# Attention by pairs of heads in halves of the matrix array, with the row maximum subtracted inside the second score product

## The chip, the cores and the metric

The kernel runs on one core of one Trainium2 chip. The metric is device time in microseconds; the kernel before takes 984.76 us (median of 3 runs, 983.75 to 986.17).

## The reference, cut to what matters

All tensors are float32. Two batches of 8 heads, 1152 keys, head dimension 64; q is pooled by pairs of rows to 576 queries per head. The weights arrive as float64.

```python
def _attn_ref(q, k, v):                       # q, k, v: (2, 8, 1152, 64)
    q_pool = q.reshape(B, H, S // 2, 2, D).mean(axis=3)
    scores = (1.0 / np.sqrt(D)) * np.matmul(q_pool, k.transpose(0, 1, 3, 2))
    scores = scores - np.max(scores, axis=-1, keepdims=True)
    attn = np.exp(scores)
    attn = attn / (np.sum(attn, axis=-1, keepdims=True) + 1e-09)
    return np.matmul(attn, v)

x = attention, heads side by side             # (1152, 512)
x = np.maximum(x @ w_in, 0) ** 2 @ w_out      # 2048 hidden units
out = ((x @ w_a) * (x @ w_b)) @ w_out2        # 1536 hidden units
```

## The kernel before

One program in two stages on one core: the attention (`attention`, L199 to L476), then the two feed-forward blocks (`mlp1`, `mlp2`), which the change leaves alone. Products are made in float32r (one pass of the matrix array per column) from operands split exactly into hi + lo, or in plain float32.

The attention works in 32 units; a unit is one head and half of its queries (CQ = 288 columns), over KT = 9 key tiles of 128. For a head, k and the pooled q are split into hi and lo side by side (`k_hi`, `k_lo`, `q_sum`, `q_hi`, `q_lo`, L254 to L274: ScalarE copies, GpSimd subtractions and additions), transposed by TensorE (`trans`, L276) into `kT`, `qB`, and `qC`, which is `qB` with its halves swapped by two GpSimd DMAs (L304, L305). So a full 128-row product of `kT` with `qB` and one with `qC` hold all the hi and lo terms of a score.

A unit's steps are: `scores` (L312), two float32r products per key tile into PSUM and a ScalarE copy of two key tiles to `s` in SBUF; `colmax` (L325), a VectorE reduction of all nine key tiles to `mx`, and a GpSimd all-reduce over the partitions to `gm`; `sub` (L340), three VectorE subtractions of `gm`; `expo` (L344), three ScalarE exponentials; `values` (L348), nine plain float32 products with 128 columns of weights, 64 of v and 64 ones, so that the denominators come out beside the values; `denom`, `recip`, `scale`, `x_hi`, `x_lo` (L359 to L392), the division and the hi/lo split of the result, once per two units.

The order is written out by hand: the table START (L23) for the beginning, then a loop over slots (L427) that issues, per slot s, the maximum of unit s + 2, the subtraction of s + 1, scores of s + 4, values of s. Each engine runs its instructions in this order, so an instruction that waits holds all behind it on its engine. `mx` has one buffer and `gm` two. SyncE issues the loads of k, q, v and of the raw weights in its own order.

`w_step` (L174) does one stage of the conversion of one weight piece, float64 words to hi and lo, on ScalarE, VectorE and, for the first pieces, GpSimd. In the attention, two pieces are begun early and the first NE = 4 are finished at the end. `early_mm` and `early_post` (L527, L533) make the first feed-forward products for half of the tokens inside the last slots of the attention; the stage after it begins with the tile `h` (L547).

Of the kernel before, what the change touches and what calls it, by code (L numbers as in the profile page):

```python
# [9 lines left out]
F32 = mybir.dt.float32  # L10
# [12 lines left out]
START = """  # L23
k_hi 0 1 A; q_sum 0 0 V; k_hi 0 0 V; k_hi 0 2 V; k_lo 0 0 P; q_hi 0 0 A; q_lo 0 0 V; q_sum 0 1 V; q_hi 0 1 A
k_lo 0 1 V; k_lo 0 2 P; trans 0 3 o AAA; q_lo 0 1 P; k_hi 1 * V; trans 0 0 t V; trans 0 1 o A
trans 0 4 o VAV; q_sum 1 * V; q_hi 1 * V; scores 0 0 A; load_q 2; k_lo 1 * P; scores 0 1 A; trans 1 2 o A
load_k 3; trans 0 2 o V; scores 0 2 A; load_k 2; load_v 2; scores 2 0 A; trans 1 1 t A; colmax 0 0
q_lo 1 * P; scores 0 3 A; scores 0 4 A; trans 1 0 t A; load_q 3; q_sum 2 * P; colmax 0 1; trans 1 3 o AVV
q_sum 3 * P; q_hi 2 * V; scores 2 1 A; scores 2 2 A; load_v 3; k_hi 3 * A; scores 2 3 A; k_lo 3 * P
k_hi 2 * V; q_lo 2 * V; load_q 4; trans 1 4 o AAV; k_lo 2 * P; scores 1 0 A; scores 2 4 A; trans 2 4 o AAA  # L30
sub 0 0; scores 1 1 A; scores 3 0 A; load_v 0; colmax 2; trans 2 3 o AAV; w_load 3; load_k 4; scores 1 2 A
trans 3 0 o A; q_hi 3 * V; scores 1 3 A; load_k 5; trans 3 2 o A; q_lo 3 * P; trans 2 2 t A; scores 3 1 A
sub 0 1; q_sum 4 * P; trans 2 0 o V; scores 1 4 A; expo 0 0; scores 3 2 A; sub 0 2; load_q 5; scores 4 0 A
trans 3 1 t A; expo 0 1; values 0 0; colmax 1; sub 2 0; scores 3 3 A; scores 3 4 A; trans 2 1 t A; expo 0 2
trans 3 3 o VVV; values 0 1; trans 3 4 o AAV; w_step 2; scores 4 1 A; values 0 2; k_hi 4 * A; sub 2 1
scores 4 2 A; values 0 3; k_lo 4 * P; expo 2 0; load_v 1; q_hi 4 * A; load_k 6; sub 2 2; values 0 4
q_lo 4 * P; colmax 3; sub 1 0; scores 5 0 A; sub 1 1; q_sum 5 * P; scores 4 3 A; expo 2 1; values 2 0
scores 5 1 A; expo 2 2; load_q 6; scores 5 2 A; values 2 1; scores 4 4 A; values 2 2; denom 0; scores 5 3 A
expo 1 0; scores 5 4 A; k_hi 5 * A; sub 1 2; values 2 3; values 2 4; w_step 2
"""  # L40
START_SLOT = 2


@with_exitstack
def kernel(
# [27 lines left out]
    TC = CQ // QP  # L73
# [9 lines left out]
    NU = NH * 2  # L83
# [7 lines left out]
    NE = 4  # L91
# [82 lines left out]
    def w_step(limit, hi=True):  # L174
        """One stage of one of the pieces before `limit`, not the one just worked on if there is another;
        one piece more may start."""
        limit = min(limit, len(order))
        if hi:
            w_hi()
        can = [i for i in sorted(work) if i < limit]  # L180
        if at["next"] < min(limit + 1, len(order)) and len(work) < 2:
            can.append(at["next"])
        if not can:
            return
        i = next((i for i in can if i != at["last"]), can[0])
        if i == at["next"]:
            at["next"] += 1
        w_stage(i)
# [10 lines left out]
    def attention(gs):  # L199
        with ExitStack() as es:  # L200
            qk_stack = ExitStack()
            qk = qk_stack.enter_context(tc.tile_pool(name="qk", bufs=1, side="right"))
            ap = es.enter_context(tc.tile_pool(name="ap", bufs=1))
            ps_s = es.enter_context(tc.tile_pool(name="ps_s", bufs=2, space=PSUM))
            ps_o = es.enter_context(tc.tile_pool(name="ps_o", bufs=3, space=PSUM))
            ps_t = es.enter_context(tc.tile_pool(name="ps_t", bufs=1, space=PSUM))

            idf = ap.tile([P, CQ], F32, tag="sg", bufs=2, name="idf")[:, :P]
            make_identity(nc, idf)
            idr = const.tile([P, P], F32R, name="idr")  # L210
            nc.vector.tensor_copy(idr, idf)
            eps = const.tile([P, 1], F32, name="eps")
            nc.vector.memset(eps, 1e-9)
            NV = 4
            vt = [ap.tile([P, 2 * KT + 1, D], F32, name=f"v{i}") for i in range(NV)]
            for i in range(NV):
                nc.gpsimd.memset(vt[i][:, 0::2, :], 1.0)

            kin, qin, khl, qhl, kT, qB, qC = {}, {}, {}, {}, {}, {}, {}
            st, om, sg, mx_t, xf, rs = {}, {}, {}, {}, {}, {}  # L220

            def k_tile(h):
                kin[h] = qk.tile([P, KT, D], F32, tag="kin", bufs=2, name=f"kin{h}")
                return kin[h], k[h // H, h % H].rearrange("(p t) d -> p t d", t=KT)

            def q_tile(h):
# [465 lines left out]
```

## Time and profile before

| | before |
|---|---|
| median of 3 runs | 984.76 us (983.75 to 986.17) |
| profiled execution, span | 983.4 us |
| busy: TensorE (PE) / VectorE (DVE) / ScalarE (ACT) / GpSimd (POOL) | 729.4 / 557.4 / 419.5 / 151.7 us |
| first product of the feed-forward stage proper (tile `h`) | 566.0 us |

The span runs from the first to the last instruction of one profiled execution. PE records of matmuls overlap, since products are pipelined: the duration of a record is a latency, and what a product costs in a dense stream is the distance from one start to the next. PEclk is the granted clock of TensorE, where 1.0 is 2.4 GHz and 0.5 is 1.2 GHz. A line of the profile names the source line, the engine, the operation, the tile written and the tiles read, the shape, the count, the busy time and the mean; in brackets or after the bar stands the idle time ahead of it with the work that ended it.

### The profile page before, as it was taken

How to read it: one execution, taken by the hardware profiler on the slowest of the kernel's cores; microseconds unless marked ns; L12 is line 12 of the kernel's file. 1: busy time of each engine (PE TensorE's matmuls, PEld its weight loads, DVE VectorE, ACT ScalarE, POOL GpSimd, SP SyncE). 2: the span in 40 equal slices, each digit the busy share in tenths (PEclk: the TensorE clock that was granted, in tenths of full speed). 3: DMA queues.
4: the chain of work that ended last, by engine and by line, in shares of the span. 5: the costliest groups of instructions: out<-in, count | busy, mean ns of one | idle time of the engine just before them, and what ended most of it. 6: DMA issues, size and time to landing. Idle time of an engine off the chain costs nothing. (4 is left out here: it accounts for less than half of the span.)

```text
span 983.4 us, 10073 instructions
## 1 busy us (share of the span) xinstructions
PE 729.4 (74%) x3830; PEld 659.7 (67%) x3830; DVE 557.4 (57%) x657; ACT 419.5 (43%) x769; POOL 151.7 (15%) x151
## 2 busy tenths in 40 slices
PE   6372757446366366357446899999999999999998
PEld 5362545335345255246335799999999999899987
DVE  7546474544635445455556789349756677127721
ACT  6353535345345344345332656237523454225510
POOL 3211322123123122123111222000000000000000
PEclk9696777867767767778677899999999999999999
DMA  5210502102003003001000122223213333103212
GB/s 151 83 48 1 115 24 49 24 25 58 14 24 73 0 25 72 1 12 37 0 1 0 43 86 87 87 84 108 68 62 105 110 128 117 57 22 116 77 33 65
DMA packets 57905, 56.36 MB, mean 57 GB/s; under 512 B 21024, under 2 KB 50400, under 8 KB 57856
## 3 DMA queue, kind: packets, MB, share of 16 engines
q1 hardware_dynamic: 55712, 51.88, 18.5%
q0 software_dynamic: 1920, 3.54, 1.7%
q8 instruction: 30, 0.49, 0.2%
q10 hardware_dynamic: 224, 0.30, 0.1%
q14 instruction: 19, 0.16, 0.0%
HBM read 49.81 MB, written 2.36 MB: 53 GB/s over the span
## 5 line engine op out<-in xcount | busy, mean ns | idle before, releaser
L333 DVE TENSOR_REDUCE mx<-s 128x288 f32<-128x2592 f32 (+1 forms) x32 | 146.8, 4587 | 235.0 <-POOL gm L338 234.7
L355 PE MATMUL o<-s,v 128*128 128x288 f32 x576 | 192.1, 463 | 8.2 <-ACT s L346 7.6
L321 PE MATMUL ps<-qB,kT 128*128 128x288 f32 x288 | 117.6, 419 | 100.9 <-ACT s L247 100.7
L321 PEld LDWEIGHTS ps<-qB,kT 128*128 128x128 f32 x288 | 63.9, 222 | 112.6 <-ACT s L247 107.6
L355 PEld LDWEIGHTS o<-s,v 128*128 128x128 f32 x576 | 118.2, 222 | 30.4 <-ACT s L346 8.3
L293 PE MATMUL pt<-idr,qhl 96*128 96x96 f32 x96 | 21.4, 348 | 105.6 <-POOL qhl L274 105.0
L346 ACT ACTIVATE s<-s 128x864 f32<-128x864 f32 x96 | 88.5, 924 | 25.1 <-DVE s L342 24.9
L342 DVE TENSOR_TENSOR s<-s,gm 128x864 f32<-128x864 f32 x96 | 96.3, 1057 | 2.6 <-POOL gm L338 2.6
L247 ACT COPY s<-ps 128x576 f32<-128x576 f32 (+1 forms) x160 | 91.6, 585 | 10.5 <-PE ps L322 8.1
L322 PE MATMUL ps<-qC,kT 128*128 128x288 f32 x288 | 92.5, 332 | 1.6 <-DVE qC L249 1.6
L293 PEld LDWEIGHTS pt<-idr,qhl 96*128 96x128 f32 x96 | 14.8, 182 | 116.1 <-POOL qhl L274 110.6
L168 DVE TENSOR_TENSOR wlo<-wx,whi 128x512 fp32r<-128x512 f32 x60 | 41.8, 696 | 54.6 <-ACT whi L134 54.5
L322 PEld LDWEIGHTS ps<-qC,kT 128*128 128x128 f32 x288 | 65.2, 226 | 6.1 <-DVE qC L249 1.8
L338 POOL PARTITION_ALL_REDUCE gm<-mx x32 | 38.5, 1202 | 191.9 <-issue 164.6
L134 ACT CAST whi<-wx 128x512 fp32r<-128x512 f32 x68 | 42.1, 620 | 55.9 <-DVE wx L153 55.8
L489 PE MATMUL y<-gl,whi 128*128 128x384 f32 x192 | 64.6, 337 | 1.2 <-DVE gl L479 1.2
L488 PE MATMUL y<-gh,whi 128*128 128x384 f32 x192 | 64.6, 336 | 0.0
L490 PE MATMUL y<-gh,wlo 128*128 128x384 f32 x192 | 64.6, 336 | 0.0
L247 ACT CAST qB<-pt 128x288 fp32r<-128x288 f32 x30 | 12.0, 401 | 117.2 <-PE pt L293 117.1
L490 PE MATMUL h<-xh,wlo 128*128 128x384 f32 (+1 forms) x176 | 57.6, 327 | 0.0
L488 PE MATMUL h<-xh,whi 128*128 128x384 f32 (+1 forms) x176 | 57.5, 327 | 0.0
L489 PE MATMUL h<-xl,whi 128*128 128x384 f32 (+1 forms) x176 | 57.5, 327 | 0.0
(92 smaller groups left out, 1590.2 us busy)
## 6 DMA issues: line engine op xcount, KB each, us to landing
raw<-in_moe_w_out_dram SPq DMA_DIRECT2D x28, 512.0 KB, 3.3
raw<-in_moe_w_in_dram SPq DMA_DIRECT2D x16, 512.0 KB, 3.8
raw<-in_moe_w_a_dram SPq DMA_DIRECT2D x12, 512.0 KB, 3.5
raw<-in_moe_w_b_dram SPq DMA_DIRECT2D x12, 512.0 KB, 3.5
v<-in_v_dram SPq DMA_DIRECT2D x16, 288.0 KB, 4.2
kin<-in_k_dram SPq DMA_DIRECT2D x15, 288.0 KB, 2.9
qin<-in_q_dram SPq DMA_DIRECT2D x15, 288.0 KB, 3.3
qC<-qB POOLq DMA_DIRECT2D x24, 144.0 KB, 4.3
```

Source lines behind the costliest of these rows:

```text
L134: nc.scalar.copy(w["hi"], w["x"].bitcast(F32))
L168: eng.tensor_tensor(out=lo, in0=x.bitcast(F32), in1=hi.bitcast(F32), op=ALU.subtract)
L247: nc.scalar.copy(out, in_)
L321: nc.tensor.matmul(pt[:, t - 2 * j, :CQ], w, qB[h][:, sl], start=True, stop=False)
L322: nc.tensor.matmul(pt[:, t - 2 * j, :CQ], w, qC[h][:, sl], start=False, stop=True)
L333: nc.vector.tensor_reduce(out=e, in_=st[u][:, kts].rearrange("p c q -> p q c"), op=ALU.max, axis=AX.X)
L342: nc.vector.tensor_tensor(out=s, in0=s, in1=g[:, None, :].to_broadcast([P, 3, CQ]), op=ALU.subtract)
L346: nc.scalar.activation(s[:, 3 * i:3 * i + 3, :], s[:, 3 * i:3 * i + 3, :], AF.Exp, scale=SCALE)
L355: nc.tensor.matmul(om[u][:, :CQ], w, st[u][:, t, :], start=t == 0, stop=t == KT - 1)
L488: nc.tensor.matmul(ps, lh, rh, start=i == 0, stop=False)
L489: nc.tensor.matmul(ps, lh, rl, start=False, stop=False)
L490: nc.tensor.matmul(ps, ll, rh, start=False, stop=i == n - 1)
```

## The change

A unit is now a pair of heads and half of their queries: 16 units of 288 columns, in which head 0 lives in rows 0 to 63 of the array and head 1 in rows 64 to 127 (`halves`).

Inputs: k and q of two heads are loaded beside each other, q is summed by GpSimd (`q_sum`), and TensorE transposes the float32 sums (15 transposes per pair, in 4 groups, through the one buffer `ps_x`). ScalarE copies a group out as hi, VectorE subtracts it for lo. The split before the transposition, `qC` and its DMAs are gone.

Maximum: of the hi parts alone a second set of scores is made, queries on the partitions, keys along the columns (`max_pair`: two products of 64 rows and 384 columns, one per head; the last 64 queries of both heads go together, `max_mix`). VectorE reduces each straight from PSUM, negated at the end (`max_end`). `max_row` turns the column of maxima into a row, by float32 products with the identity, and ScalarE copies it to `mrow`. This is a maximum of the hi products, not of the exact scores; the softmax is the same for any such shift.

Scores: per key tile and head four products of 64 rows: hi hi, lo hi, hi lo, and a fourth that adds the row of negative maxima. The two heads go into two PSUM banks, their products alternate. ScalarE takes the exponential straight from PSUM into `e`. GpSimd adds the first seven `e` tiles of a unit (`acc`, six additions), VectorE the last two (`e2`).

Values: plain float32 products with 64 weight columns, head 0 to partitions 0 to 63 and head 1 to 64 to 127 of one bank; the denominators come from four further products of `acc` and `e2` with ones. The division is `reciprocal` and one multiplication per unit on VectorE.

The order is one loop over units. The first weight load is issued in unit 13 (before: near 21 us), and all four `early_mm` come after the last unit. Removed: START, the slot loop, the copies of scores, `sub`, the all-reduce, the SBUF maximum.

```diff
+            ps_m = es.enter_context(tc.tile_pool(name="ps_m", bufs=2, space=PSUM))
+            ps_x = es.enter_context(tc.tile_pool(name="ps_x", bufs=1, space=PSUM))
...
+            halves = (slice(0, D), slice(D, 2 * D))
...
+            def prep(p, g):
+                if p < NPR:
+                    pt = prep_t(p, g)
+                    prep_hi(p, g, pt)
+                    prep_lo(p, g, pt)
+                    if g == 3:
+                        prep_mix(p)
...
+            def max_pair(p, j, c):
+                if p < NPR:
+                    ps = [ps_m.tile([P, 512], F32, tag="m", name=f"pm{p}_{j}{a}_{c}") for a in range(2)]
+                    for a, r in enumerate(halves):
                         nc.tensor.matmul(
+                            ps[a][:, :MC], hi[p][r, S + j * P:S + (j + 1) * P], hi[p][r, c * MC:(c + 1) * MC],
+                            start=True, stop=True,
                         )
+                    for a in range(2):
+                        colmax(p, 2 * j + a, c, ps[a])
...
-                    g = mx_t[u] = ap.tile([P, CQ], F32, tag="gm", bufs=2, name=f"gm{u}")
-                    nc.gpsimd.partition_all_reduce(g, m, P, bass.bass_isa.ReduceOp.max)
...
+            def scores(u, t):
+                p, c = divmod(u, 2)
+                ps = ps_s.tile([P, 2, 512], F32, tag="s", name=f"ps{u}_{t}")
+                kt, qt = slice(t * P, (t + 1) * P), slice(S + c * CQ, S + (c + 1) * CQ)
+                for i, (x, y) in enumerate(((hi, hi), (lo, hi), (hi, lo), (None, None))):
+                    for a, r in enumerate(halves):
+                        w, m = (x[p][r, kt], y[p][r, qt]) if x else (onez[r], mrow[u][r])
+                        nc.tensor.matmul(ps[:, a, :CQ], w, m, start=i == 0, stop=i == 3)
+                e = ex[u, t] = ap.tile([P, 2, CQ], F32, tag="e", bufs=15, name=f"e{u}_{t}")
+                nc.scalar.activation(e, ps[:, :, :CQ], AF.Exp, scale=SCALE)
...
+                        nc.tensor.matmul(
+                            po[u][r, :CQ], vin[u // 2][:, a, t, :], e[:, a, :], start=t == 0, stop=t == KT - 1
+                        )
...
+            for n in range(NU + 1):
+                p, odd = divmod(n, 2)
+                live = n < NU
+                todo = [(p + 1, 2 * odd + j, c) for j in range(2) for c in range(MX)] if live else []
...
+                for t in range(KT):
+                    if live:
+                        scores(n, t)
+                    if t == 0:
+                        sum_end(n - 1)
+                    if t in (0, 1, 3, 4):
+                        some(1)
+                    if t == 2:
+                        if live:
+                            prep(p + 2, 2 * odd)
+                        if odd:
+                            max_mix(p + 1, 0)
+                        values(n - 1, range(5))
+                    if t == 3:
+                        x_split(n - 2)
+                    if t == 5:
+                        if odd and p + 1 < NPR:
+                            max_end(p + 1, 0)
+                        if live:
+                            prep(p + 2, 2 * odd + 1)
+                        if odd:
+                            max_mix(p + 1, 1)
+                            max_mix(p + 1, 2)
+                        values(n - 1, range(5, KT))
+                        denom(n - 1)
+                        if live:
+                            max_row(n + 1)
+                        scale(n - 1)
+                    if t in (6, 7):
+                        some(1)
...
+                if n >= NU - 3:
+                    for _ in range(6):
+                        w_step(NE)
+            for f in range(NE):
+                early_mm(ps_s, f)
+                early_post(gpool, f)
```

Here `some(1)` is one `max_pair` of the next pair of heads. Ahead of the loop the inputs of pair 0 are prepared in full, with nine of its twelve `max_pair`; the other three, the three `max_mix` and two groups of pair 1 stand ahead of the scores of unit 0.

## Rows read from the trace of the kernel before

**Rows 1.** The page: granted TensorE clock in 40 slices of 24.6 us, in tenths.
```profile
PEclk9696777867767767778677899999999999999999
```
**Rows 2.** Busy time by stretch: start and end, PE, PEld, DVE, ACT, POOL, PEclk, DMA, GB/s.
```profile
60.00:536.00 476.00, 260.05 (x1184) 209.99 (x1182) 245.41 (x145) 201.20 (x355) 114.59 (x111) 0.76 0.13 30
...
610.00:984.00 374.00, 369.09 (x2044) 356.89 (x2042) 207.41 (x380) 139.89 (x264) 0.43 (x1) 1.00 0.26 82
```
**Rows 3.** Waits of VectorE and TensorE, longest first: us in total, times, longest.
```profile
DVE mx L333 <- POOL gm L338: 234.7, 29, 12.3
...
PE ps L321 <- ACT s L247: 100.7, 17, 16.1
```
**Rows 4.** Timeline of one slot in mid-attention: start, us, engine, line, operation.
```profile
295.37 4.63 DVE L333 TENSOR_REDUCE mx<-s 128x288 f32<-128x2592 f32 x1 [10.64 <-POOL gm L338]
...
313.19 1.17 POOL L338 PARTITION_ALL_REDUCE gm<-mx  x1 [6.03 <-issue]
...
314.39 4.82 DVE L333 TENSOR_REDUCE mx<-s 128x288 f32<-128x2592 f32 x1 [9.62 <-POOL gm L338]
```
**Rows 5.** Tile h, the first tile after the attention: min/median/max ns, first and last start.
```profile
L488 PE MATMUL h<-xh,whi x176: 292/334/338, 566.0 to 704.7; 128*128 128x384 f32 x144, 128*128 128x288 f32 x32
```
**Rows 6.** Timeline of TensorE, dense stretches at full clock: scores, then values.
```profile
397.13 0.29 PE L322 MATMUL ps<-qC,kT 128*128 128x288 f32 x1
397.26 0.30 PE L321 MATMUL ps<-qB,kT 128*128 128x288 f32 x1
...
550.02 4.53 PE L355 MATMUL o<-s,v 128*128 128x288 f32 x18
...
554.17 0.51 PE L488 MATMUL e<-xh,whi 128*128 128x288 f32 x1
```
**Rows 7.** Timeline at the start: six transposes with their own weights, then the next.
```profile
8.22 0.68 PE L285 MATMUL pt<-idr,khl 128*128 128x128 f32 x6
...
8.74 0.41 PE L293 MATMUL pt<-idr,qhl 96*128 96x96 f32 x3
```
**Rows 8.** Granted clock by stretch, columns as in rows 2.
```profile
20.00:24.00 4.00, 2.58 (x18) 2.21 (x18) 3.38 (x4) 3.58 (x9) 1.10 (x1) 1.00 0.66 160
...
28.00:32.00 4.00, 0.42 (x3) 0.42 (x4) 1.80 (x1) 0.00 (x0) 2.81 (x3) 0.50 0.34 116
...
64.00:68.00 4.00, 1.71 (x11) 1.25 (x10) 0.64 (x2) 2.50 (x5) 2.86 (x2) 1.00 0.25 62
...
50.00:75.00 25.00, 18.25 (x95) 14.77 (x94) 11.24 (x11) 14.21 (x25) 5.66 (x4) 0.96 0.16 41
```
**Rows 9.** Groups by shape, VectorE and ScalarE: busy us, mean ns.
```profile
L333 DVE TENSOR_REDUCE mx<-s 128x288 f32<-128x2592 f32 x31 | 143.4, 4627 | 234.7 <-POOL gm L338 234.7
L333 DVE TENSOR_REDUCE mx_end<-s 128x288 f32<-128x864 f32 x1 | 1.1, 1130 | 0.0
L249 DVE CAST kT<-pt 128x384 fp32r<-128x384 f32 x3 | 1.7, 554 | 2.5 <-PE pt L285 2.5
L509 DVE TENSOR_TENSOR g<-r 128x576 f32<-128x576 f32 x4 | 3.1, 764 | 1.1 <-ACT r L507 1.1
L373 DVE RECIPROCAL sg<-sg 128x288 f32<-128x288 f32 x16 | 31.2, 1947 | 0.0
L507 ACT ACTIVATE r<-e 128x576 f32<-128x576 f32 x4 | 2.6, 640 | 0.2 <-PE e L490 0.2
L365 ACT ACTIVATE sg<-o,eps 64x288 f32<-64x288 f32 x16 | 8.0, 498 | 0.4
```
**Rows 10.** Timeline of GpSimd, the same shape early and beside VectorE's work.
```profile
7.47 1.41 POOL L261 TENSOR_TENSOR khl<-kin,khl 128x576 fp32r<-128x576 f32 x1
...
302.25 1.91 POOL L261 TENSOR_TENSOR khl<-kin,khl 128x576 fp32r<-128x576 f32 x1 [6.91 <-issue]
```
**Rows 11.** DMA issues: count, KB each, median us from issue to landing.
```profile
raw<-in_moe_w_in_dram SPq DMA_DIRECT2D x16, 512.0 KB, 3.8
...
v<-in_v_dram SPq DMA_DIRECT2D x16, 288.0 KB, 4.2
```

More of the change, by code (lines that the diff above doesn't have):

```diff
@@ L18 @@
 PSUM = bass.MemoryType.PSUM
[L23 to L41, printed above, removed]
 @with_exitstack
@@ L267, in q_hi @@
[L267 to L284 removed]
+            ones = const.tile([P, D], F32, name="ones")
@@ new lines, in attention @@
+            nc.vector.memset(ones, 1.0)
+            first = const.tile([P, P], F32, name="first")
+            nc.vector.memset(first, 0.0)
+            for r in (0, D):
+                nc.vector.memset(first[r:r + 1], 1.0)
+            onez = const.tile([P, P], F32R, name="onez")
+            nc.vector.tensor_copy(onez, first)
+            qm = [const.tile([P, P], F32R, name=f"qm{i}") for i in range(2)]
+            for t in qm:
+                nc.vector.memset(first, 0.0)
+                nc.vector.tensor_copy(t, first)
@@ new lines, in q_sum @@
+            def q_sum(p, eng=None):
+                if p < NPR:
+                    x, y = (qin[p][:, :, :, i * D:(i + 1) * D] for i in range(2))
+                    qs[p] = kq.tile([QP, QT, 2, D], F32, tag="qs", bufs=2, name=f"qs{p}")
+                    out = qs[p].rearrange("p t a d -> p a t d")
+                    (eng or nc.gpsimd).tensor_tensor(out=out, in0=x, in1=y, op=ALU.add)
+            groups = [[("k", t) for t in range(4)], [("k", t) for t in range(4, 8)],
+                      [("k", 8)] + [("q", t) for t in range(3)], [("q", t) for t in range(3, 6)]]
@@ new lines, in attention, with prep_t @@
+            starts = [0, 512, 1024, 1024 + P + 3 * QP, NB]
+            def prep_t(p, g):
+                if p not in hi:
+                    hi[p] = kq.tile([P, NB], F32R, tag="hi", bufs=3, name=f"hi{p}")
+                    lo[p] = kq.tile([P, NB], F32R, tag="lo", bufs=3, name=f"lo{p}")
+                pt = ps_x.tile([P, 512], F32, tag="x", name=f"pt{p}_{g}")
+                c0 = 0
+                for what, t in groups[g]:
+                    src, n = (kin[p][:, t], P) if what == "k" else (qs[p][:, t], QP)
+                    nc.tensor.matmul(pt[:, c0:c0 + n], src, idf[:n, :n], is_transpose=True, start=True, stop=True)
+                    c0 += n
+                return pt
@@ new lines, in denom @@
+            def denom(u):
+                if not 0 <= u < NU:
+                    return
+                pt = ps_x.tile([P, 512], F32, tag="x", name=f"den{u}")
+                for i, x in enumerate((acc[u], e2[u])):
+                    for a, r in enumerate(halves):
+                        nc.tensor.matmul(pt[r, :CQ], ones, x[:, a, :], start=i == 0, stop=i == 1)
+                sg[u] = ap.tile([P, CQ], F32, tag="sg", bufs=2, name=f"sg{u}")
+                nc.scalar.activation(sg[u], pt[:, :CQ], AF.Identity, bias=eps)
@@ L398, in attention @@
+            load_k(0)
+            load_q(0)
             load_k(1)
             load_q(1)
[L400 removed]
+            warm = ps_x.tile([P, 512], F32, tag="x", name="warm")
             for i in range(NWARM):
[L402 to L407 removed]
@@ new lines, in attention @@
+                nc.tensor.matmul(warm[:, :P], idf, idf, is_transpose=True, start=True, stop=True)
+            q_sum(0, nc.vector)
+            for g in range(4):
+                pt = prep_t(0, g)
+                prep_hi(0, g, pt)
+                prep_lo(0, g, pt)
+            prep_mix(0)
+            q_sum(1)
+            load_v(0)
+            for j in range(3):
+                for c in range(MX):
+                    max_pair(0, j, c)
+            max_end(0, 0)
+            for g in range(2):
+                prep(1, g)
```

351 lines of the change are left out of this document (133 added, 218 removed).

## The prediction

> **What bounds the kernel now.** I read the clock and the stretches first, then the waits, then one slot of the timeline. The clock row [rows 1] parts the run in two: some 23 slices with changing clock, then 17 at full clock. In the second part TensorE is busy 369 of 374 us at 1.00 [rows 2]: that stage is bound by products, and the change leaves it alone. In the attention TensorE is busy 260 of 476 us, VectorE 245, ScalarE 201, at a mean clock of 0.76 [rows 2]: nothing is full, so a chain of waits sets the pace. The waits name it: VectorE waits 234.7 us for the all-reduce `gm` in front of its next reduction, and TensorE 100.7 us for ScalarE's copies [rows 3]. One slot shows how: the reduction of 4.63 us at 295.37 ends at 300.0, the all-reduce ends at 314.36, the next reduction starts at 314.39 [rows 4]. Each unit goes once through reduction, all-reduce, subtraction and exponential; in the pauses TensorE falls to half clock [rows 8]. The stage after it starts at 566.0 [rows 5] and needs 983.4 - 566.0 = 417.4 us. So the question is when the new attention lets `h` start.
>
> **What goes.** The all-reduce with its 234.7 us of VectorE waits, the subtractions, the copies of scores. VectorE then waits on no GpSimd work except, through the denominators, on `acc`. What is late next is worked out for one new unit (two heads, 288 queries, 16 of them), in place of two old units.
>
> **Prices of products.** A float32r product of 288 columns starts 0.13 us after the one before, though its own record is 0.29 long [rows 6]: 288 columns at 2.4 GHz plus some 10 ns. Nine plain float32 products take from 550.02 to 554.17 [rows 6], with what trails some 0.48 us each, four passes of 288 columns. Six transposes of 128 columns with their own weights take 8.74 - 8.22 = 0.52, 0.087 us each [rows 7].
>
> No row shows two products in halves of the array, and here lies most of the doubt. A pair of 64-row score products costs between 0.131 us (side by side) and 0.262 (one after the other). Both load 128 weight columns, and the fastest row of a load with its product is 0.087, so I take 2 x 0.087 = 0.172. A pair of value products in column halves costs between 0.48 and 0.96; they load 64 columns each, so I take 0.48. I take side by side because in rows 6 each product's weight load already hides beside the running product, and halves share no rows, columns or PSUM partitions that would tie them. The Trainium skill ("TensorE: Matmul & The Clock Gate", "Measured speedup vs the span model") gives 3.07 for four row tiles and 2.38 for three column tiles, less than full packing; no run here shows it. By some 1.6 for two halves, an estimate from that page, score pairs would cost 0.164 and value pairs 0.60, and the total would be some 16 us more.
>
> **A unit on TensorE.** Scores: 9 key tiles x 4 pairs x 0.172 = 6.2 us. Maximum: 6 pairs of 384 columns x 0.17 = 1.0, and 1.5 mixed ones on average, 0.25. Transposes: 7.5 x 0.087 = 0.65; these read plain float32, so up to four passes, 2.6, are open; the nearest row is a transpose, so I take 0.65. Values: 9 x 0.48 = 4.3. Denominators: 2 x 0.48 = 1.0. Row of maxima: 288 float32 columns, 0.48. Sum 13.9 us. Between 64-row, full and 64-column products the array changes about six times per unit. A record outlasts its spacing by 0.29 - 0.13 = 0.16 us [rows 6]; if each change waits for that tail, 6 x 0.16 = 1.0 us; bounds 0 and 1.0, I take 1.0. The Trainium skill ("TensorEngine Tiling (Array Packing)", "Key Properties") says that a change of mode drains the array, without a figure; no row shows one, and without the term the total is 15 us less.
>
> **A unit on the other engines.** VectorE: 13.5 reductions of 384 columns from PSUM, each between 0.50 (1130 x 384/864) and 0.69 (4627 x 384/2592); the cast of that size from PSUM takes 0.554, so 0.56, 7.6 us. Two `lo` of 288 to 512 columns, 1.2; last sum 0.76; reciprocal 1.95; scale 0.45 [rows 9]. Sum 12.0. ScalarE: nine exponentials x 0.64 = 5.8, two `hi` 1.1, `mrow`, denominators and `x_split` some 1.4 [rows 9]: 8.3. GpSimd: six additions of 576 columns between 1.41 and 1.91 [rows 10], 8.5 to 11.5, and about 2 for `q_sum`, `x_split` and `prep_mix`: 10.5 to 13.5. So none of these is the bound by its sum. GpSimd's additions are hidden by the rest of the unit; below a period of 13.5 us that cover is gone and `denom` would wait for `acc`.
>
> **What waits.** TensorE runs in order, and `ps_m` has two buffers: each `max_pair` waits until VectorE has reduced the one before (1.1 us), and the scores queue behind. I walk from `denom`. `max_row` needs `ps_x`, so it waits for ScalarE's copy of the denominators: 0.25 + 0.5 = 0.75. VectorE then does reciprocal and scale, 2.4 us, ahead of the `max_pair` of tile 6, so that of tile 7 waits about 1.5. In the next unit the last sum (0.76, after the ninth exponential) and two reductions come together: tile 1 waits 1.2. After the first values, tiles 3 and 4 wait 0.6. Sum 4.05. Odd units hold three mixed reductions more, 1.7 us, about half of it seen: 0.45 on average. **Period: 13.9 + 1.0 + 4.05 + 0.45 = 19.4, say 19.5 us**, with side-by-side bounds of 16.5 (0.131 per score pair, no changes of mode, fewer waits) and 22 (slow transposes, reductions of 0.69). The longest pause is near 2 us. Clock: in stretches of 4 us with 2.58 and with 1.71 busy the granted clock was 1.00, over 25 us at 73% busy it was 0.96, and in 4 us with 0.42 busy 0.50 [rows 8]. The unit above is busy for 14 of 19.5, so I take full clock.
>
> **Start and end.** Hidden on both sides before, bare now. k and q of two heads are loaded in 256-byte pieces, as v is (4.2 us to land [rows 11]); all of pair 0 and its q sum are there by about 12 us. Four groups through the single `ps_x` cost transposes, copy, subtraction, 1.9 us each with the first half done: 18. Nine `max_pair` x 1.1: 28. Two groups of pair 1, the row, then 3 x 1.1 + 3 x 0.56, and two more groups: scores of unit 0 start at 37 (bounds 32 and 42; before, at 9). Unit 0 has no values: 11. Then 15 x 19.5 = 292.5. After unit 15 its values, denominators and division: 6. The weights are first loaded in unit 13: ScalarE and VectorE, in order, wait for a load (3.8 us [rows 11]) with exponentials and reductions behind them, and 12 stages of conversion join VectorE's queue: 8 us (bounds 3 and 12); before, this lay in pauses. The 96 products of `early_mm` now stand alone: 96 x 0.131 = 12.6. `h` starts at 37 + 11 + 292.5 + 6 + 8 + 12.6 = 367. SyncE: a load of q waits for the q sum on GpSimd, of v for the values of the pair before last, the next k behind it; each is needed a period or more later, so nothing is added. The first stretch of the feed-forward stage finds the same four pieces converted and stays as it is.
>
> **Sum.** Span 367 + 417.4 = 784.4. The median stands 1.4 above the span (984.76 against 983.4). **Forecast 786 us.**
>
> **Rivals.** (a) *The halves run one after the other.* The change then doesn't do what it says: scores 9.4, maxima 2.3, values 8.6, denominators 1.9, row 1.0, transposes 0.65 make 23.9; with changes of mode 1.0 and waits of some 1.8 (VectorE has more time) 26.7. 37 + 16 + 15 x 26.7 + 6 + 8 + 12.6 = 480, total 899. If only the scores run side by side, 25 per unit and 870; if only the values, 22.3 and 829. For it: no row shows halves side by side. Against it: what I took above. (b) *The array's clock falls to half, halves side by side.* Against it speak the stretches at 1.00 that were half busy [rows 8]; for it, that every product of this attention but transposes and mixes fills only half of the array, and no row shows what clock such products get. Products that are bound by columns double: about 28 per unit, 922 in all. (c) *Slower: half clock and halves one after the other.* Place: TensorE's own 23.9 us per unit become 48, with little wait left, 50. 37 + 32 + 750 + 27 = 846 for `h`, 1265 in all. It decides from a period of (566 - 37 - 11 - 27)/15 = 32.7 us on; above that the new kernel is slower. The stretch at 0.50 [rows 8] shows that the state exists; the stage in which TensorE is busy all the time was at 1.00 throughout [rows 2].
>
> **How the numbers follow.** Forecast 0.60, one or both kinds of halves in series 0.26, half clock side by side 0.06, slower 0.06, about the same 0.02. A measurement of this kernel can tell about 0.3% from no change, so (a), (b) and the forecast are all faster: 0.92 faster, 0.02 same, 0.06 slower. Range: from 737 (period 16.5, start 37, end 24) up through the partial cases to just past 899; what is left out is most of (b), (c) and the tail of (a), some 0.2. So 735 to 905; the forecast's own range is 737 to 826.
>
> **What the changed profile would show.** `h` first starts near 367; unit to unit 19.5 us; PEclk near 1.0 from the start. A pair of score products on the two heads starts within some 0.17 us of the next pair, value records pair up every 0.48. VectorE's waits name TensorE's `pm` tiles, TensorE's name VectorE's reductions, none of length names GpSimd. If value products of one head follow each other at 0.48 and the period is above 25, (a) holds; PEclk near 0.5 means (b) or (c). If `denom` waits for GpSimd for long, my additions were too cheap: they would have to cost 2.9 us each.

## The result and the profile after

The changed kernel takes 772.71 us (median of 4 runs, 770.97 to 772.95) against 984.25 us for the kernel before on the same chip (4 runs, 982.11 to 986.17): a ratio of 0.784, interval 0.782 to 0.786. The forecast was 786. The profiled execution below has a span of 769.1 us.

The page of the changed kernel: busy time by engine, then the granted TensorE clock in 40 slices of 19.2 us, in tenths.

```profile
PE 708.7 (92%) x4822; PEld 604.3 (79%) x4822; DVE 443.0 (58%) x790; ACT 303.3 (39%) x562; POOL 174.4 (23%) x148
...
PEclk8579999999999998899999999999999999999999
```

After three slices the clock stays up, but for two slices of 0.8 (288 to 326 us); before, it changed through the whole attention [rows 1]. The views by stretch and by tile give the terms of the sum (columns as in rows 2 and rows 5).

```profile
0.00:42.60 42.60, 27.92 (x103) 18.29 (x103) 21.01 (x47) 5.43 (x9) 2.97 (x9) 0.64 0.51 115
42.60:56.00 13.40, 11.40 (x104) 9.41 (x105) 7.46 (x15) 7.06 (x12) 10.40 (x9) 0.86 0.34 78
56.00:276.00 220.00, 193.21 (x1775) 130.92 (x1771) 131.77 (x230) 90.64 (x165) 119.67 (x101) 1.00 0.17 40
276.00:334.00 58.00, 45.47 (x391) 29.84 (x391) 28.16 (x46) 24.48 (x44) 27.49 (x21) 0.88 0.20 60
```
```profile
L512 PE MATMUL h<-xh,whi x176: 292/334/338, 353.9 to 491.1; 128*128 128x384 f32 x144, 128*128 128x288 f32 x32
```

`h` starts at 353.9 instead of 566.0 [rows 5], and 769.1 - 353.9 = 415.2 us follow, nearly the 417.4 of before. In the steady stretch TensorE is busy 193 of 220 us at clock 1.00, where it was busy 260 of 476 at 0.76 [rows 2].

GpSimd's first addition of a unit comes once per unit, so its starts measure the units; here those of units 1 and 12 to 15 (start, us, line, tile, shape, idle time ahead):

```profile
58.67 1.41 POOL L355 TENSOR_TENSOR acc<-e,e 128x576 f32<-128x576 f32 x1 [2.31 <-ACT e L352]
...
263.23 1.41 POOL L355 TENSOR_TENSOR acc<-e,e 128x576 f32<-128x576 f32 x1 [3.13 <-ACT e L352]
280.41 1.42 POOL L355 TENSOR_TENSOR acc<-e,e 128x576 f32<-128x576 f32 x1 [3.17 <-ACT e L352]
302.01 1.49 POOL L355 TENSOR_TENSOR acc<-e,e 128x576 f32<-128x576 f32 x1 [6.62 <-ACT e L352]
321.83 1.49 POOL L355 TENSOR_TENSOR acc<-e,e 128x576 f32<-128x576 f32 x1 [5.22 <-ACT e L352]
```

Eleven units from 58.67 to 263.23 make 18.6 us each; units 12, 13 and 14 last 17.2, 21.6 and 19.8. The waits of TensorE and VectorE (us in total, times, longest):

```profile
PE pm L302 <- DVE mm L295: 21.7, 37, 0.9
PE ps L350 <- ACT e L352: 9.1, 8, 3.8
PE mr L335 <- ACT sg L384: 8.4, 14, 0.6
...
DVE mm L295 <- PE pm L302: 37.0, 27, 3.4
```

The 234.7 us on the all-reduce [rows 3] are gone, and no engine waits at length for GpSimd; TensorE and VectorE now wait for each other through `ps_m`. Part of one unit on TensorE (start, us, line, tile, shape, count; "x2" is the pair of heads):

```profile
200.50 0.72 PE L335 MATMUL mr<-idf,nm 128*64 128x96 f32 x12 [0.60 <-ACT sg L384]
201.15 0.40 PE L350 MATMUL ps<-hi 64*128 64x288 f32 x2
201.39 0.29 PE L350 MATMUL ps<-hi,lo 64*128 64x288 f32 x2
201.52 0.30 PE L350 MATMUL ps<-lo,hi 64*128 64x288 f32 x2
...
201.79 0.34 PE L302 MATMUL pm<-hi 64*128 64x384 f32 x2
201.97 0.29 PE L350 MATMUL ps<-hi 64*128 64x288 f32 x2
...
203.55 0.90 PE L302 MATMUL pm<-hi 64*128 64x384 f32 x2 [0.89 <-DVE mm L295]
204.02 0.40 PE L350 MATMUL ps<-hi 64*128 64x288 f32 x1
...
209.11 2.65 PE L372 MATMUL po<-e,vin 128*64 128x288 f32 x20
211.68 0.40 PE L350 MATMUL ps<-hi 64*128 64x288 f32 x2
...
301.44 0.61 PE L350 MATMUL ps<-hi 64*128 64x288 f32 x2 [3.74 <-ACT e L352]
302.70 4.17 PE L372 MATMUL po<-e,vin 128*64 128x288 f32 x20
...
335.58 4.59 PE L372 MATMUL po<-e,vin 128*64 128x288 f32 x36 [0.85 <-DVE xf L397]
340.00 0.66 PE L382 MATMUL den<-acc,ones 128*64 128x288 f32 x4
```

Two things are to be read here. Both heads' products start together, and the next pair 0.13 us later: the price of one full product [rows 6], for two halves. And five pairs of value products (20 records, two for each plain float32 product) take 2.57 us, 0.51 per pair, with the change to the next kind of product in it; nine pairs in a row, at the end, take 4.42 us (335.58 to 340.00), 0.49 per pair. The rows at 301.44 and 302.70 belong to unit 13, where the weight conversion begins: a 3.74 us wait, and behind it the same 20 value records take 4.17 instead of 2.65 us; the granted clock was 0.50 from 301.4 to 302.7 us and 0.62 over these records.

### The profile page after: what moved, and what is told of

Read it like the earlier page. It is cut to its first block, busy times and chain, and to the rows that moved or that the text cites. A ratio compares the mean times of both kernels' runs of the same rounds, so it can differ in the third digit from the quotient of the medians.

```text
span 769.1 us, 11886 instructions
## 1 busy us (share of the span) xinstructions
PE 708.7 (92%) x4822; PEld 604.3 (79%) x4822; DVE 443.0 (58%) x790; ACT 303.3 (39%) x562; POOL 174.4 (23%) x148
## 4 chain that ended last, share of the span: by engine, by line
PE 83%; DVE 11%; ACT 4%; issue 1%; DMA 1%; SPq 0%; DVEq 0%; ACTq 0%
PE po L372 10%; PE pm L302 6%; PE ps L350 6%; PE y L512 4%; PE y L514 4%; PE y L513 4%; PE h L512 4%; PE h L513 4%; PE h L514 4%; DVE sg L395 4%; DVE mm L295 4%; PE b L514 3%; PE a L513 3%; PE a L514 3%; PE b L513 3%; PE b L512 3%
## 5 line engine op out<-in xcount | busy, mean ns | idle before, releaser
L352 ACT ACTIVATE e<-ps 128x576 f32<-128x576 f32 x144 | 91.9, 650 | 113.5 <-PE ps L350 112.3
L357 POOL TENSOR_TENSOR acc<-acc,e 128x576 f32<-128x576 f32 x80 | 112.5, 1407 | 89.5 <-ACT e L352 88.0
L295 DVE TENSOR_REDUCE mm<-pm 128x1 f32<-128x384 f32 x192 | 98.0, 551 | 39.7 <-PE pm L302 37.0
L302 PE MATMUL pm<-hi 64*128 64x384 f32 x192 | 66.5, 428 | 24.4 <-DVE mm L295 21.7
L372 PE MATMUL po<-e,vin 128*64 128x288 f32 x576 | 80.1, 425 | 0.8 <-DVE xf L397 0.8
L350 PE MATMUL ps<-hi 64*128 64x288 f32 x288 | 63.3, 354 | 10.3 <-ACT e L352 9.1
L350 PE MATMUL ps<-hi,lo 64*128 64x288 f32 x288 | 52.9, 297 | 0.0
L350 PE MATMUL ps<-mrow,onez 64*128 64x288 f32 x288 | 52.8, 297 | 0.0
L350 PE MATMUL ps<-lo,hi 64*128 64x288 f32 x288 | 52.7, 295 | 0.0
L138 DVE SCALAR_TENSOR_TENSOR wx<-raw,wx 128x512 int32<-128x512 int32 x68 | 47.1, 692 | 2.4
```

What stands on the lines that cost most here:

```text
L138: nc.vector.scalar_tensor_tensor(out=x, in0=high.bitcast(I32), scalar=-(2 ** 31), in1=x, op0=ALU.bitwise_and, op1=ALU.bitwise_or)
L295: nc.vector.tensor_reduce(out=mm[p][:, i, c:c + 1], in_=ps[:, :MC], op=ALU.max, axis=AX.X)
L302: nc.tensor.matmul(ps[a][:, :MC], hi[p][r, S + j * P:S + (j + 1) * P], hi[p][r, c * MC:(c + 1) * MC], start=True, stop=True,)
L350: nc.tensor.matmul(ps[:, a, :CQ], w, m, start=i == 0, stop=i == 3)
L352: nc.scalar.activation(e, ps[:, :, :CQ], AF.Exp, scale=SCALE)
L357: nc.gpsimd.tensor_tensor(out=acc[u], in0=acc[u], in1=e, op=ALU.add)
```

## The experiments

Each number is a run's median; ratios are to the kernel before on the same chip. That kernel took 980.8 to 984.5 us on the chips used, so runs on different chips that lie 4 us or less apart are not told apart here. "Unit" means the mean distance between the same step of two successive units.

**1. Are the halves side by side?** The same products, issued one head after the other.

```diff
-                for i, (x, y) in enumerate(((hi, hi), (lo, hi), (hi, lo), (None, None))):
-                    for a, r in enumerate(halves):
+                for a, r in enumerate(halves):
+                    for i, (x, y) in enumerate(((hi, hi), (lo, hi), (hi, lo), (None, None))):
```

> The changed kernel, with the four score products of head 0 ahead of the four of head 1, where the changed kernel alternates the heads; nothing else moves. Theory: the products of the two heads run side by side only because they alternate. TensorE starts them in program order, so by head only the last of head 0 and the first of head 1 lie beside each other: 7 starts of 0.13 us per key tile in place of 4, +0.4 x 144 tiles = 57 us, less what falls into the waits for VectorE: 805 to 830 us. Rival: the alternating products already run one after the other, or the weight loads are the bound; then the order makes no difference: 773 us.

Measured: 771.74 us, no difference from 772.71. The trace says why (TensorE's timeline of this kernel):

```profile
205.43 0.29 PE L350 MATMUL ps<-hi,lo 64*128 64x288 f32 x1
205.47 0.29 PE L350 MATMUL ps<-hi 64*128 64x288 f32 x1
205.56 0.29 PE L350 MATMUL ps<-lo,hi 64*128 64x288 f32 x1
205.60 0.29 PE L350 MATMUL ps<-hi,lo 64*128 64x288 f32 x1
```

The `hi` product at 205.47 is the first of head 1 and stands behind all four of head 0 in the program, yet it starts before the third of them, at 205.56. The instructions of the compiled program stand in the order of the source, so it was TensorE that started the other half's products early, and the two halves ran beside each other anyway. My premise, that products start in program order, fell, and this run can't show what a series costs. That the halves overlap is shown by the rows: each half starts a product every 0.13 us. The Trainium skill ("TensorE: Matmul & The Clock Gate", "The mechanism") says that matmuls keep program order in start and end, without reordering; these four rows differ from that, and the measurement decides.

```diff
-                for t in ts:
-                    e = ex.pop((u, t))
-                    for a, r in enumerate(halves):
+                for a, r in enumerate(halves):
+                    for t in ts:
+                        e = ex[u, t]
```

> The changed kernel, with the value products of a group (five, then four key tiles) all for head 0 and then all for head 1. Theory (column halves run side by side while they alternate): 9 + 7 starts of 0.48 us per unit in place of 9, +3.4 us x 16 = 54 us; VectorE has nothing to do in these stretches, so little of it is hidden: 815 to 827 us. Rival (column halves in series already): 773 us.

Measured: 811.36 us (ratio 0.825), below the range by 4. Here the order counts: the group of 20 value records is longer.

```profile
209.06 4.15 PE L372 MATMUL po<-e,vin 128*64 128x288 f32 x20
...
218.77 0.46 PE L382 MATMUL den<-acc,ones 128*64 128x288 f32 x1
219.01 0.41 PE L372 MATMUL po<-e,vin 128*64 128x288 f32 x1
```

4.15 against 2.65 us, and at its end later denominators run beside the last values. So the column halves run side by side when they alternate; the alternation is worth 811 - 773 = 39 us here.

**2. Where does the gain come from?** The kernel before without its all-reduce.

```diff
-                    mx_t[u] = ap.tile([P, CQ], F32, tag="mx", bufs=1, name=f"mx{u}")
+                    mx_t[u] = ap.tile([P, CQ], F32, tag="gm", bufs=2, name=f"gm{u}")
...
-                    nc.gpsimd.partition_all_reduce(g, m, P, bass.bass_isa.ReduceOp.max)
```

> The kernel before without the GpSimd all-reduce: every partition subtracts the maximum of its own keys, written to the two buffers of gm (so the maximum over the partitions is left out); all else stays, the halves are not used. Theory: the chain through the all-reduce set the pace before, and what bounds the attention without it is VectorE's own work, 4.63 + 3.0 + 1.2 = 8.8 us per old unit and some waits: 32 x 9.3 + 45 = 343 for the end of the attention, 760 to 800 us in all, so nearly all of the gain would come from the all-reduce and little from the halves. Rival: other waits of the old order (the shared PSUM buffers, the hand-written start, half clock) take its place: above 850 us, and the halves and the direct exponential carry a good part of the gain.

Measured: 746.46 us (ratio 0.759 [0.756, 0.761]). By stretch:

```profile
60.00:300.00 240.00, 207.78 (x1092) 170.22 (x1090) 237.02 (x135) 186.75 (x338) 70.60 (x77) 0.93 0.22 53
```

VectorE is busy 237 of 240 us: with the chain cut, its reductions and subtractions bound the old attention. It lands 14 us below the range, and 26 us below the changed kernel. This kernel leaves out the maximum over the partitions, each of which subtracts its own, so its results are not the reference's and any full maximum would add to its time. As a bound it says that the removal of the all-reduce is worth more than the whole gain, and that the other parts, taken together, need not have brought any of it.

What made the all-reduce dear is not its own 1.17 us. In the kernel before, GpSimd stands idle some 6 us ahead of an all-reduce (6.03 at 313.19 [rows 4]) and again ahead of the first other instruction behind one (6.91 at 302.25 [rows 10]), waiting for nothing that the profile shows (total, times, longest):

```profile
POOL gm L338 <- issue: 164.6, 27, 8.9
```

All gaps of this kind come to some 360 us there and to 0.2 in the run without the all-reduce. So they come with the changes between the all-reduce and GpSimd's ordinary instructions; what happens in them is not shown. TensorE's longest wait before, 105.0 us for GpSimd's `qhl`, which the prediction passes over, is gone in that run too.

Next, no maximum at all, in the changed kernel and in the kernel before (there the exponential also goes straight from PSUM). Both leave out what keeps the exponential in range for large scores.

```diff
@@ changed kernel
-                    ps = [ps_m.tile([P, 512], F32, tag="m", name=f"pm{p}_{j}{a}_{c}") for a in range(2)]
...
-                        colmax(p, 2 * j + a, c, ps[a])
+                    pass
@@ kernel before
-                copy(e, st[u][:, 2 * j:2 * j + len(kts), :], pt[:, :len(kts), :CQ])
+                nc.scalar.activation(st[u][:, 2 * j:2 * j + len(kts), :], pt[:, :len(kts), :CQ], AF.Exp, scale=SCALE)
```

> The changed kernel without the second set of scores: no maximum products, no reductions, the row of maxima is zero (so the maximum is left out). Theory: the period of 18.5 us is TensorE's own 13.2 us plus the waits that max_pair brings between TensorE and VectorE; without both, TensorE's 11.7 and the wait for the denominators, about 13 per unit, and some 12 us off the start: 772 - 15 x 5.5 - 12 = 675 us (665 to 690). Rival: the waits come from elsewhere (the single buffer for transposes and denominators, ScalarE's exponentials): only the 1.5 us of products go, 735 to 750 us.

> The kernel before without any maximum (no reduction, no all-reduce, no subtraction: that part is left out); the exponential is taken straight from PSUM in place of the copy. It stands against the changed kernel without its maximum (705 us, 14.8 us per pair unit): both then have scores, exponentials and values alone, one with full 128-row products, one in halves. Theory 1: the halves bring nothing on TensorE, since the full products held hi and lo side by side: 6.5 + 0.6 = 7.1 us per old unit, 14.2 per pair; 32 x 7.2 + 45 = 275 for the end of the attention, 690 to 705 us. Theory 2: the value products with ones beside the values (9 x 0.48 per head, twice those in halves) make it clearly longer than the halves, 17 us per pair and more: above 740.

Measured: 705.38 us for the changed kernel, between the two ranges, and 683.85 us for the kernel before, 6 below the lower end of the first theory. In the latter TensorE is busy without a gap:

```profile
60.00:260.00 200.00, 200.00 (x1150) 171.02 (x1149) 46.70 (x45) 133.11 (x262) 68.29 (x79) 1.00 0.25 61
```

Without the maximum the halves were the slower kernel, by 22 us. So the maximum, with the copies and subtractions that it brought, cost 984 - 684 = 300 us in the kernel before and costs 773 - 705 = 67 in the changed one, while the rest went from 684 to 705: the gain lies in the cheaper maximum. The changed one without its maximum still has waits that my walk did not hold:

```profile
PE ps L341 <- ACT e L343: 19.6, 47, 3.8
```

TensorE has two score buffers of two banks, a tile's products take 0.53 us and its exponential 0.65, so every second tile waits. Its unit is 14.8 us. Leaving out the maximum frees two banks of PSUM, enough for a third score buffer:

```diff
-            ps_s = es.enter_context(tc.tile_pool(name="ps_s", bufs=2, space=PSUM))
-            ps_m = es.enter_context(tc.tile_pool(name="ps_m", bufs=2, space=PSUM))
+            ps_s = es.enter_context(tc.tile_pool(name="ps_s", bufs=3, space=PSUM))
```

> The maximum is left out as in the run no_max (the softmax is shifted by zero), and the two PSUM banks that its products no longer need become a third buffer of two banks for the scores. In the run no_max TensorE waits 19.2 us between 42 and 288 us, 45 times, for ScalarE's exponential to free a score buffer. Theory (the score buffers are the term that my walk through the waits lacked): most of these 19 us go, the unit falls from 14.8 to 13.7 us, and the time from 705 to 685 to 693. Rival (the wait is ScalarE's rate: a pair of tiles takes 1.3 us of exponentials and TensorE 1.06 us, so a third buffer only moves the wait): 700 to 706. If the theory holds, this also tells what the array halves are worth at their best against the kernel before without its maximum, 683.9: nothing.

Measured: 672.69 us (671.94 to 673.44; ratio 0.683), lower than both ranges. The waits and the stretch of its steady units:

```profile
PE ps L340 <- ACT e L342: 3.8, 2, 2.2
```
```profile
56.00:236.00 180.00, 168.18 (x1799) 121.77 (x1797) 69.35 (x87) 98.40 (x191) 136.40 (x110) 0.99 0.26 68
```

Units 1 to 12 take 13.1 us each instead of 14.7, some 19 us together. Another 11 of the 32.7 lie between unit 13 and `h`, where the clock had fallen in the run before: over units 13 and 14 it was 0.89 there (218 to 256 us) and 1.00 here (197 to 228 us). The theory holds in kind, though the gain is about twice what it gave (12 to 20), and its last sentence falls: with three score buffers the halves are 683.85 - 672.69 = 11 us faster than the kernel before without its maximum; with two they were 22 slower. The two kernels differ in start, denominators and weights as well, so not all of this need be the halves. In the changed kernel all eight banks are taken, two of them by the maximum.

**3. Can the waits be taken out?** First, the `max_pair` steps placed further apart, between portions of the values (`spread`); then the weight conversion from unit 4 on (`early_weights`); then a start in which scores of unit 0 don't wait for the preparation of pair 1 (`start`); then all three together.

```diff
-                    if t in (0, 1, 3, 4):
...
+                        values(n - 1, range(4))
+                        some(1)
+                        values(n - 1, range(4, 5))
```

> The changed kernel with the same instructions in another order: two of a unit's six max_pair and the mixed ones are moved in between the value products (where VectorE had nothing to do), the one of tile 0 stands ahead of the last sum, the one of tile 4 ahead of the transposes; max_row is preceded by a mixed product. Theory: the period of 18.6 us holds about 4 us in which TensorE waits for VectorE through the two ps_m buffers; with a reduction's length of other products between any two, the period is TensorE's own 13.2 us, the wait for the denominators and for the exponentials: 15 us, the total 722 (710 to 735). Rival: VectorE itself, with 12.1 us per unit plus what it waits for the denominators, or ScalarE's exponentials behind the scores hold the period: 17.5 us and more, above 753.

Measured: 746.82 us (ratio 0.761), between the two ranges: half of what was expected. The wait for `mm` falls from 21.7 to 3.1 us, and the one for `e` grows from 9.1 to 13.0:

```profile
PE ps L350 <- ACT e L352: 13.0, 22, 3.8
...
PE pm L302 <- DVE mm L295: 3.1, 10, 0.8
```

The unit falls from 18.6 to 16.8 us. By these waits `ps_m` was the larger of two places where TensorE was held; the score buffers are the other.

```diff
-                if n >= NU - 3:
+                if n >= 4:
+                    w_step(NE)
+                if n == NU:
```

> The changed kernel with the first three weight loads in unit 2 and one stage of the conversion in each unit from 4 on, in place of six stages at the end of units 13 to 16. The prediction put 8 us (3 to 12) on the late loads and stages; in the trace units 13 and 14 take 21.6 and 19.8 us where others take 18.6, which is 4.2 us. Theory: that much comes back, 768 (766 to 770). Rival: a stage costs as much in each unit as it did at the end, no change: 773.

Measured: 771.17 us, no difference that counts, as the rival said. GpSimd's first additions of units 7 to 9 and 13 to 15:

```profile
173.40 1.41 POOL L355 TENSOR_TENSOR acc<-e,e 128x576 f32<-128x576 f32 x1 [3.16 <-ACT e L352]
194.13 1.84 POOL L355 TENSOR_TENSOR acc<-e,e 128x576 f32<-128x576 f32 x1 [1.36 <-ACT e L352]
216.74 1.42 POOL L355 TENSOR_TENSOR acc<-e,e 128x576 f32<-128x576 f32 x1 [3.18 <-ACT e L352]
...
290.36 1.41 POOL L355 TENSOR_TENSOR acc<-e,e 128x576 f32<-128x576 f32 x1 [3.15 <-ACT e L352]
309.50 1.40 POOL L355 TENSOR_TENSOR acc<-e,e 128x576 f32<-128x576 f32 x1 [3.63 <-ACT e L352]
324.37 1.41 POOL L355 TENSOR_TENSOR acc<-e,e 128x576 f32<-128x576 f32 x1 [1.72 <-ACT e L352]
```

Units 13 and 14 fall from 21.6 and 19.8 to 19.1 and 14.9, 7.4 us together, and units 7 and 8 grow from 18.6 to 20.7 and 22.6, 6.1 together: the conversion costs much the same in either place.

```diff
-            for g in range(2):
-                prep(1, g)
...
+                if n == 0:
+                    for t in range(KT):
+                        scores(0, t)
+                        if t < 3:
+                            max_pair(0, 3, t)
+                        if t in (1, 2):
+                            prep(1, t + 1)
```

> The changed kernel with another start: pair 0's transposes and maxima go through the four banks of the scores (one reduction for both heads), groups of k ahead of the q sum, and what unit 0 does not need (three max_pair, the mixed ones, two groups of pair 1) is made between unit 0's scores. The prediction put 37 us ahead of the scores of unit 0, the trace shows 42.6. Theory: the start is a chain through few PSUM buffers at half clock, about 24 us would do, unit 0 gets 2 to 3 us longer: 773 - 16 = 757 (752 to 762). Rival: the loads of q and k bound it: no more than 4 us, 769.

Measured: 767.3 us, 5 below the changed kernel instead of 16, and hardly told apart by the ratios (0.782 against 0.784). The time is near the rival's, but not for its reason: scores begin at 27.1 instead of 42.6, but unit 0 now takes 22.5 instead of 12.7 us: the same preparations, and at little more than half clock.

```profile
27.10:49.60 22.50, 20.40 (x120) 14.89 (x118) 11.79 (x24) 8.73 (x15) 8.84 (x8) 0.58 0.24 53
```

> The changed kernel with the order of maxima, the early weights and the other start together. Theory: the three are separate terms of the sum and add up: 773 - 51 - 4 - 16 = 702 (690 to 715). Rival: with the period of 15 us GpSimd's additions or VectorE (12.1 us, and the weight stages) become the bound and part is lost: 720 to 740.

Measured: 745.58 us (743.17 to 749.17), the same as `spread` alone and above both ranges: the savings do not add up. By GpSimd's first additions, unit 1 comes 9 us earlier than in `spread` (49.43 against 58.42) and units 13 and 14 are 8 us shorter together, but units 5 to 11, which now hold the weight stages, are 14 us longer together.

Then a finer weave: values in portions of one or two key tiles, with `max_pair` between them, so that TensorE always has work while VectorE or ScalarE catches up; and the same with the new start.

```diff
+                        some(1)
...
+                        values(n - 1, range(2))
...
+                        values(n - 1, range(2, 3))
+                        some(1)
+                        values(n - 1, range(3, 4))
```

> The changed kernel with the same instructions in a finer order: after the scores of each key tile from the third on stand one or two value products and one max_pair, and the denominators before the last two score tiles. In the run with the maxima moved (746.8, 16.8 us per unit) TensorE no longer waited for VectorE but up to 0.8 us per score tile instead of 0.53, because the two score buffers are handed to ScalarE and back (0.65 per exponential). Theory: with a value product between score tiles that wait is covered too: 15 us per unit, 718 (710 to 730). Rival: the changes between 64-row and 64-column products, some 18 per unit in place of 6, cost 0.1 to 0.2 each and eat it: 740 to 750.

> The order of the kernel weave and the other start (which alone gave 5 us): the two terms are apart, so 5 us below weave; if weave's order changes what unit 0 hides, no difference.

Measured: 760.07 and 751.84 us. `weave` lies above both ranges, with a unit of 17.7 us; with the other start it is 8 us faster, where 5 or none was expected. In `weave` TensorE hardly waits for the others (4.5 us in all for `pm`, 5.0 for `pm_x`, 8.5 for `ps`), but its products cost more:

```profile
200.26 0.40 PE L350 MATMUL ps<-hi 64*128 64x288 f32 x2
200.50 0.29 PE L350 MATMUL ps<-hi,lo 64*128 64x288 f32 x2
...
200.76 0.30 PE L350 MATMUL ps<-mrow,onez 64*128 64x288 f32 x2
200.98 0.71 PE L372 MATMUL po<-e,vin 128*64 128x288 f32 x4
201.62 0.45 PE L302 MATMUL pm<-hi 64*128 64x384 f32 x2
202.00 0.71 PE L372 MATMUL po<-e,vin 128*64 128x288 f32 x4
202.63 0.40 PE L350 MATMUL ps<-hi 64*128 64x288 f32 x2
```

The last score pair starts 0.22 us ahead of the values instead of 0.13, the first after a change 0.24 ahead of the next (200.26 to 200.50), and a value pair on its own takes 0.64 (200.98 to 201.62) instead of 0.49. From one tile of scores to the next (200.26 to 202.63) 2.37 us pass. The tile (0.53), two value pairs (0.98) and a `max_pair` (0.18) make 1.69; the other 0.68 go to four changes between row halves and column halves, some 0.17 us each. The Trainium skill ("TensorEngine Tiling (Array Packing)", "Key Properties") says that a change of tiling mode drains the array; the rows agree and give the price.

## Why the prediction was right, step by step

**What held.** The all-reduce chain set the pace of the kernel before: taking it alone away brings 238 us. What is late next is TensorE's own products and the hand-over through `ps_m`: its waits name VectorE's reductions, not GpSimd. The halves run side by side (pairs at 0.13 and 0.49, against rival (a)), and the clock stays up in the steady units (against (b) and (c)). GpSimd's additions took 1.407 us, the lower bound, so their cover was never in question. The changes of the array cost what was taken, 1.0 per unit (six of some 0.17). Last values (335.0 to 341.1) and `early_mm` (341.1 to 353.9) came as worked out, 6 and 12.8.

**Right by luck, or for a wrong reason.** The weights' 8 us are near the 7.4 by which units 13 and 14 shrink in the run that moves them, but the mechanism was another: in this stretch ScalarE and VectorE wait for no load. The 3.74 us wait of TensorE in unit 13 comes from conversion stages on ScalarE that stand ahead of the exponentials (296.75 to 300.84) and wait for VectorE. And one reason given for side by side was not right: the row halves of the scores do share the array's columns and the PSUM partitions (they differ in rows and banks), and the column halves share rows. The rows show them side by side all the same.

**Terms that were mis-sized.** The period was 18.6, not 19.5:

- Score pairs: 0.172 taken, 0.13 measured, the lower bound, 1.5 us per unit too much. The weight loads of two row halves did not add up as I had them do.
- Value pairs were right, 0.49 against 0.48; the 0.51 in a group of five, and the 0.65 of the row of maxima (200.50 to 201.15) where 0.48 was taken, hold the change behind them. So the products make 13.9 - 1.5 = 12.4.
- Waits: 18.6 - 12.4 - 1.0 leaves 5.2, where 4.05 and 0.45 for odd units stood. By the rows, `max_row` waited 0.60 of the 0.75 and `max_pair` up to 0.9. TensorE's idle time is only (21.7 + 9.1 + 8.4)/16 = 2.4 us per unit, so the larger part of the 5.2 lies inside records; one such place is a `max_pair` after a wait, which takes 0.47 (203.55 to 204.02) instead of 0.18 (201.79 to 201.97). The rest of it I have not traced. The wait of scores for a buffer that ScalarE has to free was not in the walk; the run with a third buffer shows that it is real where the maximum is out.

Outside the steady units:

- Start: 42.6 against 37, for the most part an error of addition. Up to the end of the nine `max_pair` the sum came out (27.66 in TensorE's timeline against 28), with two errors that cancelled: the preparation was done at 15.66 instead of 18, and the nine took 12.0 instead of 9.9. The steps listed behind them (two groups, the row, three `max_pair`, three mixed ones, two groups) add up to 13.1 by the prediction's own prices, where the step from 28 to 37 leaves 9. In the trace they take 14.9, since they ran at a clock of 0.50: a `max_pair` came every 1.33 us (35.24 to 36.57) instead of 1.1, a group of transposes every 2.5 (27.66 to 30.18) instead of 1.9.
- Unit 0: 12.7 against 11, at clock 0.86.
- Units 12 to 15: they have fewer pairs ahead to prepare, and I had counted them as full ones. With the weights 4 x 19.5 + 8 = 86 stood in the sum, and they took 75 (unit 15 ends at 335.0).

The sum: units 1 to 11 were 10 us too long in it, units 12 to 15 11, the rest 2; start and unit 0 7 too short. That makes 16 by these rounded terms, and the span was 769.1 instead of 784.4, 15 less. Errors of both signs partly cancelled, and the total is nearer than its largest terms.

**What the prediction had not asked.** It priced the new attention and never asked what the old one would cost with its all-reduce out. That kernel, 746 us, leaves out the maximum over the partitions, but it has neither halves nor a direct exponential and is faster than the changed one; and with no maximum on either side the kernel in halves is the slower one, 705 against 684, unless the freed banks are used. So halves and the direct exponential did not earn the gain, the new way to a maximum did. The changed kernel pays for it with about 100 us (773 against 673 with no maximum and the freed banks used): TensorE products, VectorE reductions, the longer start and the lost score buffer together. The best kernels with a full maximum that were run are `all_three` and `spread`, with 745.6 and 746.8 us, not told apart and 3% below the changed one. Whether the row halves of the scores cost twice as much when they are truly in series was not tried, since issuing them in that order does not make it so.

## What to carry to other kernels

Before giving a gain to a new layout, cut the old bottleneck out of the old kernel and time that: here it alone was worth more than the whole change. When an accumulator is added to PSUM, ask which buffer it displaces, because without the maximum two score buffers against three turned the array halves from a loss of 22 us into a gain of 11. And fill TensorE's waits with coarse portions of other work: each change between row and column halves costs, so the finer weave lost what it saved.

## What the runs showed of the hardware

- Products of the two row halves started 0.13 us after the pair before, the same spacing as one full-array product of 288 columns, and plain float32 pairs in column halves 0.49 us apart (nine in 4.42 us), against 0.46 for a full-array product (nine in 4.15 us [rows 6]): two halves were packed fully or nearly so.
- TensorE started products of the other row half ahead of earlier ones in the program (205.47 before 205.56). Over eight score products issued head after head that hid the order wholly; over ten value products only in part (4.15 against 2.65 us).
- Changing between products of 64 rows and of 64 columns cost some 0.17 us each time (0.68 us for four in `weave`).
- A wait of 3.74 us in TensorE was followed by 20 value records at 4.17 instead of 2.65 us, at a granted clock of 0.62.
- GpSimd stood idle some 6 us ahead of an all-reduce (6.03) and again ahead of the first ordinary instruction behind one (6.91), some 360 us in all in the kernel before and 0.2 in the run without the all-reduce.
